# A graph message kernel: comparison ramps and slot masks moved to a PSUM bank, and the transposed one-hots moved to ScalarE

## The chip, the cores and the metric

The kernel runs on one core of one Trainium2 chip. The metric is the device time of one execution in microseconds (us): the median of 3 runs. The engines are called as the profile calls them: PE is TensorE's matmul (PEld its weight loads), DVE is VectorE, ACT is ScalarE, POOL is GpSimd, SP is SyncE, which here only issues DMAs.

## The reference

A graph of 12500 nodes with 64 features each has 800000 edges, each with 4 features of its own, a source and a target node. Every edge makes a message, and the messages are summed by target:

```
h_src = x[src]
h_dst = x[dst]
m_in = jnp.concatenate([h_src, h_dst, e_attr], axis=-1)
h = _silu(m_in @ w1 + b1)            # 132 -> 128
msg = h @ w2 + b2                    # 128 -> 64
return _segment_sum(msg, dst, N)
```

The kernel sums h by target and applies w2 once per node at the end; b2 is multiplied by the number of edges of the node.

## The kernel before, in words

**Tables.** x times the source part of w1 is written to DRAM as a table Atab (one row of two fp16 halves, 512 bytes, per node); x times the target part stays in SBUF as Btab, in buckets of 128 nodes (R = 98 buckets). S, also in SBUF, collects the sums by node.

**Two kinds of work.** The edges come in 16 portions. Each portion is first sorted by bucket of the target (the functions `rank` and `place`, generators that hand out work in small pieces), into rows of CS = 16 edge slots in a DRAM buffer buf. Then the main loop `run` goes over batches of CB = 32 rows (512 slots, two buckets' pieces of 256), one per step, 1590 steps in all. A step belongs to one batch n and works ahead in stages: loads of codes (11 steps ahead), index lists (`sources`, 8), gathers from Atab (`gather`, 6, four indirect DMAs of 128 rows each on GpSimd's queue), the target codes spread over all partitions (`spread`, 4), `targets` (2), `marks` (1), and for n itself `pre` and `silu`, one step later `onehot`, two steps later `seg` and `accum`. While the batches of one portion go through `run`, the sorting of the next portions is put between them as filler: each generator yields a cost in ns with each piece, and `filler` deals the pieces out over the steps and half-steps by these costs. Before the first step the first portion is ranked and placed without anything beside it.

**rank** compares the bucket of each edge with a ramp (ohb, L421, against the ramp iob), counts on TensorE, and gets each edge's place by matmuls into a PSUM tile rx, from which `slots` takes the maximum over the buckets (L529, slT).

**place** works on groups of GT = 20 columns of 128 edges, in pieces of SUB = 5 columns. For each block of 80 columns `records` makes the payload pay (three bf16 parts of the features, the target in its bucket plus one, the source) and per edge the row lo and the slot in the row. For each group the slot becomes a mask over the 16 slots, q, in three passes (L839 shift left, L842 arithmetic shift right by 31, L845 to 16 bits as qh). Per piece, mk is the payload masked by slot: L860 (qh AND pay, 520 32-bit elements) and L864 (q AND the 32-bit pair of target and source, 80 elements). The one-hots oh of the row (L869, one instruction of 384 elements per column, against the ramp io3) and co (L856) go to TensorE as weights; mk is the moving operand, and the product pl holds the rows, which ScalarE copies out (carry, L891; cb, L894) and GpSimd scatters to buf (L878). Later in `rank` the row numbers are found with comparisons stp (L710), also against io3.

**The step.** In `pre` TensorE adds into one PSUM bank px: the gathered rows times idA (L1078), the edge features times WE (L1082), and the target's row of Btab picked by a one-hot oT (L1084). oT is [128, 1024] for two batches: the target codes in the slots, compared on VectorE with the partition number plus one and multiplied by a scale (L1055). `silu` (ScalarE, L1103) gives h; `marks` gives the one-hots the other way round, ob (L1064, against the ramp io1), which ScalarE copies to fp32 (sg, L1099); `seg` (L1111) sums h by target into another px bank, and `accum` (L1119, twice per step, the second as VectorE's last instruction of the step) adds this to S.

**Order.** Each engine works in program order. `in_order` fixes the order of every engine as traced: per step `sources`, `gather`, `spread`, `marks`, `targets`, `seg(n-2)`, `onehot(n-1)`, `pre(n)`, `silu(n)`, then the fillers with TensorE's filler work at four places, with `accum(n-2, 0)` before and `accum(n-2, 1)` after the last of them. Tile buffers rotate: a tile's allocation waits until the user of the same buffer some allocations before has finished. px has 4 banks here, and takes two allocations per step, first `seg(n-2)`, then `pre(n)`; rx and pl have 2 banks each, which makes 8.

```
def targets(n):
    w = st[n]["w"]
    if w:
        oT = st[n]["ot"][:, :512 * w]
        VE.tensor_scalar(oT, oT, iop1[:, 0:1], inv, op0=OP.is_equal, op1=OP.mult)
```

Of the kernel before, what the change touches and what calls it, by code (L numbers as in the profile page):

```python
# [82 lines left out]
def tile_mpnn(ctx, tc, x, e_attr, src, dst, w1, b1, w2, b2, out, portions):  # L83
# [50 lines left out]
    sht = cst.tile([128, CS], I32, name="sht")  # L134
    GP.iota(sht, pattern=[[-1, CS]], base=31, channel_multiplier=0)
    one_i = cst.tile([128, 1], I32, name="one_i")
    GP.memset(one_i, 1)
    ones_b = cst.tile([128, 1], BF, name="ones_b")
# [112 lines left out]
    Btab = cst.tile([128, R, 2, 128], FH, name="Btab")  # L251
    scl = cst.tile([128, 2], F32, name="scl")
    inv = scl[:, 1:2]
# [4 lines left out]
    def tables():  # L258
# [12 lines left out]
        for i, (a, e) in enumerate(zip(qs, qs[1:])):  # L271
# [5 lines left out]
                         apply_absolute_value=True)  # L277
        mp = ps.tile([128, 512], F32, name="px", bufs=4)
        for i in range(3):
# [9 lines left out]
        VE.tensor_scalar(mi[:, 4:5], mi[:, 5:6], -1.0, float(254 << 23), op0=OP.mult, op1=OP.add)  # L289
        sp = ps.tile([128, 512], F32, name="px", bufs=4)  # L290
        PE.matmul(sp[:, 0:2], ones_f[0:1, :], mr[0:1, 4:6], start=True, stop=True)
        VE.tensor_copy(scl, sp[:, 0:2])
        VE.tensor_scalar(idA, idf, inv, None, op0=OP.mult)
        yield 0
        for c0 in range(0, R, 4):
            cn = min(4, R - c0)
            pt = ps.tile([128, 512], F32, name="px", bufs=4)
            for i in range(cn):
# [4 lines left out]
            for i in range(0, cn, 2):  # L303
                m = min(2, cn - i)
                pab = ps.tile([128, 2, 2, 128], F32, name="px", bufs=4)
                for u in range(m):
                    PE.matmul(pab[:, u].rearrange("p a h -> p (a h)"),
                              xt[:65, (i + u) * 128:(i + u + 1) * 128],
                              wab.rearrange("p a h -> p (a h)"), start=True, stop=True)
                for a, hi, lo in ((0, Sh[:, c0 + i:c0 + i + m, :H], Sh[:, c0 + i:c0 + i + m, H:2 * H]),  # L310
                                  (1, Btab[:, c0 + i:c0 + i + m, 0], Btab[:, c0 + i:c0 + i + m, 1])):
                    SC.activation(hi, pab[:, :m, a, :], AF.Copy, scale=scl[:, 0:1])
                    VE.scalar_tensor_tensor(lo, pab[:, :m, a, :], scl[:, 0:1], hi, op0=OP.mult, op1=OP.subtract)
# [434 lines left out]
    def records(p, c0, cn):  # L748
# [6 lines left out]
        def twice(f):  # L755
# [43 lines left out]
                                op0=OP.add, op1=OP.add)  # L799
        tw = wk.tile([128, PW], I32, name="tw")  # L800
        VE.tensor_tensor(tw[:EP, :cn], one_i[:EP].to_broadcast([EP, cn]), kk[:EP, 1, :cn],
                         op=OP.logical_shift_left)
        yield 270
        p["rec", c0] = (pay, lo, tw)
        yield 1200

    def place(p):
# [19 lines left out]
        for c0 in range(0, cols, PW):  # L827
            cn = min(PW, cols - c0)
            if c0 == 0:
                yield from records(p, 0, cn)  # L830
            pay, lo, tw = p.pop(("rec", c0))
            nxt = records(p, c0 + PW, min(PW, cols - c0 - PW)) if c0 + PW < cols else iter(())
            subs = sum(-(-min(GT, cn - go) // SUB) for go in range(0, cn, GT))
            for g in range(c0 // GT, -(-(c0 + cn) // GT)):
                go = g * GT - c0
                gt = min(GT, cn - go)
                assert gt > SUB
                q = wk.tile([128, GT, CS], I32, name="q", bufs=1)
                VE.tensor_tensor(q[:EP, :gt], tw[:EP, go:go + gt].unsqueeze(2).to_broadcast([EP, gt, CS]),  # L839
                                 sht[:EP].unsqueeze(1).to_broadcast([EP, gt, CS]), op=OP.logical_shift_left)  # L840
                yield 735
                VE.tensor_scalar(q[:EP, :gt], q[:EP, :gt], 31, None, op0=OP.arith_shift_right)  # L842
                yield 430
                qh = wk.tile([128, GT, CS], I16, name="qh", bufs=1)
                VE.tensor_copy(qh[:EP, :gt], q[:EP, :gt])  # L845
                yield 300
                for s0 in range(0, gt, SUB):
# [3 lines left out]
                    if s0 + sn == gt:  # L851

                        if s0 < 2 * SUB:
# [6 lines left out]
                    VE.tensor_tensor(  # L860
                        mk[:EP, :sn, CS:].rearrange("p s (f j) -> p s f j", f=NU),
                        qh[:EP, s0:s0 + sn].bitcast(I32).unsqueeze(2).to_broadcast([EP, sn, NU, CS // 2]),
                        pi[:, :, :NU].unsqueeze(3).to_broadcast([EP, sn, NU, CS // 2]), op=OP.bitwise_and)
                    VE.tensor_tensor(mk[:EP, :sn, :CS], q[:EP, s0:s0 + sn],  # L864
                                     pi[:, :, NU:].to_broadcast([EP, sn, CS]), op=OP.bitwise_and)
                    yield 800
# [34 lines left out]
                    def mm(g=g, s0=s0, mk=mk, oh=oh, gt=gt, sn=sn, co=co, at=at):  # L901
                        if s0 == 0:
# [7 lines left out]
                        pa, pb = box[0]  # L910
                        terms = [(oh[:EP, i], mk[:EP, i].bitcast(BF))
                                 for i in range(sn)]
# [35 lines left out]
    def bucket_table(k, t0):  # L948

        tp = ps.tile([128, 512], F32, name="px", bufs=4)  # L950
        ns = 2 * k + 1
# [99 lines left out]
    def targets(n):  # L1051
        w = st[n]["w"]
        if w:
            oT = st[n]["ot"][:, :512 * w]
            VE.tensor_scalar(oT, oT, iop1[:, 0:1], inv, op0=OP.is_equal, op1=OP.mult)  # L1055

# [15 lines left out]
    def pre(n):  # L1072
        s = st[n]
        v = regs(n, ET.PE)
        pr = ps.tile([128, 512], F32, name="px", bufs=4)

# [28 lines left out]
    def seg(n):  # L1105

        s = st[n]
        bank = ps.tile([128, 512], F32, name="px", bufs=4)
# [189 lines left out]
    def turn_sums(b0):  # L1298

        if b0 < R:  # L1300
            bn = min(4, R - b0)
            tp = ps.tile([128, 512], F32, name="px", bufs=4)
            for i in range(bn):
# [53 lines left out]
```

## Time and profile before

| | us |
|---|---|
| median of 3 runs | 9934.91 |
| lowest and highest | 9934.45, 9937.09 |
| the profiled execution | 9947.36 |
| its span, first to last instruction | 9945.5 |
| first gather / last gather of `run` starts | 423.3 / 9880.1 |
| main loop per step, 1590 steps | 5.95 |

A group line of the profile gives line, engine, operation, output<-inputs, shapes and count, then the busy time in us and the mean of one in ns, then the engine's idle time before these instructions and what ended most of it. "issue" is a pause in which the engine waited for nothing that the profile shows. A line of the busy times by stage gives for each stretch its length, then busy us and count of PE, PEld, DVE, ACT and POOL, the granted TensorE clock, the share of the DMA engines and GB/s; asked for one source line, it gives that line's engine alone. A timeline line gives start, duration, engine, line, operation and, in square brackets, the idle time before it. The mean granted TensorE clock of the execution is 0.874.

### The profile page before, as it was taken

What the parts mean: (1) busy time and instruction counts of PE and PEld (TensorE: products, weight loads), DVE (VectorE), ACT (ScalarE), POOL (GpSimd) and SP (SyncE); (2) the same over time, 40 slices, a digit from 0 to 9 for tenths busy, and PEclk for the clock granted to TensorE, in tenths of its full rate; (3) what the DMA queues carried; (4) which work ended last, traced back from release to release, by engine and by line L of the source; (5) the groups of instructions that cost most, each with busy time, mean ns of one, the idle gap of its engine ahead of it and who ended that gap; (6) DMA issues with size and microseconds to landing.
All of it is one profiled execution on the core that took longest, in us unless ns stands there. A gap on an engine that the chain in (4) does not pass through costs nothing. (4 is left out here: it accounts for less than half of the span.)

```text
span 9945.5 us, 220568 instructions
## 1 busy us (share of the span) xinstructions
PE 7609.8 (77%) x72601; PEld 6386.5 (64%) x72601; DVE 7087.5 (71%) x24824; ACT 2096.2 (21%) x3956; POOL 7372.0 (74%) x7039
## 2 busy tenths in 40 slices
PE   7877787887887778777877777777787787776666
PEld 5666666766766667666666666666566666665555
DVE  8978788977996678777677776676687876553222
ACT  1122121221212212222222222222122222222222
POOL 1477777777767777777777777777777777777775
PEclk8988899988988888888888888888898888887777
DMA  1254444544444444444444444454454444544554
GB/s 47 49 93 85 84 81 85 91 78 88 73 79 80 79 88 81 79 90 81 80 88 79 77 90 82 78 93 81 73 96 80 88 77 74 85 80 82 88 86 76
DMA packets 3266044, 806.39 MB, mean 81 GB/s; under 512 B 2979003, under 2 KB 3056216, under 8 KB 3264952
## 3 DMA queue, kind: packets, MB, share of 16 engines
q1 hardware_dynamic: 3038362, 348.44, 28.5%
q0 software_dynamic: 223584, 441.40, 17.1%
q8 instruction: 640, 10.49, 0.5%
q14 instruction: 452, 3.70, 0.1%
q10 hardware_dynamic: 3006, 2.36, 0.1%
HBM read 720.89 MB, written 89.76 MB: 82 GB/s over the span
## 5 line engine op out<-in xcount | busy, mean ns | idle before, releaser
L1092 POOL DMA_INDIRECT ga<-Atab,ix x6360 | 6653.2, 1046 | 1987.1 <-issue 1553.6
L920 PE MATMUL pl<-mk,oh 128*128 128x240 bf16 x18750 | 2401.4, 286 | 124.0 <-DVE oh L869 117.8
L1078 PE MATMUL px<-ga,idA 128*128 128x512 f16 x3180 | 1094.4, 430 | 1685.5 <-DMA ga<-Atab,ix 1137.0
L1103 ACT ACTIVATE h<-px 128x512 f32<-128x512 f32 x1590 | 949.4, 597 | 6756.3 <-PE px L1084 6552.7
L920 PEld LDWEIGHTS <-oh 128*128 128x128 bf16 x18750 | 1917.8, 105 | 459.4 <-DVE oh L869 198.9
L1111 PE MATMUL px<-h,sg 128*128 128x129 f32 x12720 | 1951.0, 300 | 111.4 <-ACT sg L1099 71.1
L1111 PEld LDWEIGHTS px<-h,sg 128*128 128x128 f32 x12720 | 1726.3, 210 | 130.6 <-ACT sg L1099 75.4
L869 DVE TENSOR_SCALAR oh<-io,lo 128x384 bf16<-128x384 bf16 x6250 | 1744.1, 323 | 0.1
L1084 PE MATMUL px<-Btab,oT 128*128 x12720 | 1535.7, 240 | 0.3
L1119 DVE TENSOR_TENSOR S<-S,px 128x129 f32 x3180 | 896.3, 282 | 859.6 <-PE px L1111 785.5
L1078 PEld LDWEIGHTS <-idA 128*128 128x128 bf16 x3180 | 324.6, 102 | 1805.5 <-issue 1614.6
L1082 PE MATMUL px<-WE,pts 65*128 65x128 bf16 x6360 | 1371.6, 241 | 0.8 <-DMA pts<-buf 0.8
L1084 PEld LDWEIGHTS <-oT 128*128 128x128 bf16 x12720 | 1150.8, 110 | 246.5 <-issue 90.9
L529 DVE TENSOR_REDUCE slT<-rx 128x5 f32<-128x490 f32 x1250 | 822.1, 660 | 479.9 <-PE rx L521 474.9
L860 DVE TENSOR_TENSOR mk<-qh,pay 128x520 int32<-128x520 int32 x1250 | 867.2, 694 | 385.6 <-PE pl L920 375.0
L1099 ACT ACTIVATE sg<-ob 128x512 f32<-128x512 bf16 x1590 | 992.2, 624 | 102.5 <-DVE ob L1064 102.2
L878 POOL DMA_INDIRECT buf<-cb,idx x626 | 687.7, 1099 | 294.6 <-issue 131.2
L1082 PEld LDWEIGHTS <-pts 65*128 65x128 bf16 x6360 | 686.7, 108 | 235.0 <-issue 77.8
L521 PEld LDWEIGHTS <-selB 82*128 82x128 bf16 x6250 | 437.4, 103 | 284.5 <-issue 160.8
L1064 DVE TENSOR_TENSOR ob<-io,d 128x1024 bf16<-128x1024 bf16 x795 | 551.3, 693 | 84.1 <-DVE d L1062 1.4
L517 PE MATMUL rx<-ohb,triO 128*128 128x490 bf16 x1250 | 498.7, 399 | 115.8 <-DVE slT L529 80.6
L521 PE MATMUL rx<-bT,selB 82*128 82x98 bf16 x6250 | 511.8, 216 | 15.3 <-DVE bT L503 14.2
(233 smaller groups left out, 5638.0 us busy)
## 6 DMA issues: line engine op xcount, KB each, us to landing
oT<-dsc SPq DMA_DIRECT2D x795, 256.0 KB
ga<-Atab,ix POOLq DMA_INDIRECT x6360
pts<-buf SPq DMA_DIRECT2D x2385, 24.0 KB
buf<-zero SPq DMA_DIRECT2D x272, 120.0 KB
psc<-buf SPq DMA_DIRECT2D x795, 4.0 KB
dsc<-buf SPq DMA_DIRECT2D x795, 2.0 KB
pld<-psc SPq DMA_DIRECT2D x795, 4.0 KB
el<-in_e_attr_dram SPq DMA_DIRECT2D x76, 160.0 KB
```

Of the source, the lines that this page charges most:

```text
L521: PE.matmul(xp[:EP, i * R:(i + 1) * R], selB[:NR, s_:s_ + 1].to_broadcast([NR, EP]), bT[g][:NR, :R], start=False, stop=i == n - 1)
L860: VE.tensor_tensor(mk[:EP, :sn, CS:].rearrange("p s (f j) -> p s f j", f=NU), qh[:EP, s0:s0 + sn].bitcast(I32).unsqueeze(2).to_broadcast([ ...
L869: VE.tensor_scalar(oh[:EP, i], io3[:EP], lo[:EP, go + s0 + i:go + s0 + i + 1], None, op0=OP.is_equal)
L920: PE.matmul(pa[:, u, :CS * PC] if u < 2 else pb[:, :CS * PC], oh_[:, u * 128:(u + 1) * 128], mv, **fl)
L1078: PE.matmul(pr.rearrange("p (t h) -> p t h", t=4), idA, s["ga"][:, :, u * H:(u + 1) * H], start=u == 0, stop=False)
L1082: PE.matmul(pr[:, sl], s["pts"][:, sl], WE, start=False, stop=False)
L1084: PE.matmul(pr[:, sl], s["oT"][:, sl], Btab[:, ds(v[t // 2], 1), u, :], start=False, stop=t == 3 and u == 1)
L1092: GP.indirect_dma_start(out=ga[:, t, :], out_offset=None, in_=Atab, in_offset=bass.IndirectOffsetOnAxis(ap=s["ix"][:, t:t + 1], axis=0))
L1099: SC.activation(sg, s["ob"][:, :4].rearrange("p t h -> p (t h)"), AF.Copy)
L1103: SC.activation(hs[n % 3][:, :, :H], st[n]["pr"].rearrange("p (t h) -> p t h", t=4), AF.Silu)
L1111: PE.matmul(s["so"][t // 2], s["sg"][:, t * 128:(t + 1) * 128], hs[n % 3][:, t, :], start=t % 2 == 0, stop=t % 2 == 1)
L1119: VE.tensor_tensor(S[:, ds(v[u], 1), :], S[:, ds(v[u], 1), :], s["so"][u].unsqueeze(1), op=OP.add)
```

## The change

- The ramps io3, io1 and iob move from SBUF tiles to one PSUM bank, fix: ramps by partition are made on VectorE and transposed there by TensorE, once at the start. Every instruction that compares with a ramp (ohb, stp, co, oh, ob) then reads it from PSUM.
- The slot mask is made in another way. m16 is a bf16 one-hot of the slot over 16 slots. For the masking of 32-bit pairs, half is a 32-bit mask over 8 pairs of slots: a comparison of the slot's upper bits (e8) times a value that covers the lower or the upper 16 bits. half is written to the same bank fix. The first instruction on mk masks with half; the second multiplies target and source, as bf16, with m16, 160 elements instead of 80.
- `records` makes the operands for this (s2, hv) in place of the power of two, tw.
- `targets` makes oT on ScalarE, in two passes over the 1024 elements: the absolute value of code minus partition number minus one, then a rectifier that leaves the scale where that is 0, and 0 elsewhere.
- The px tiles share 3 banks instead of 4, since fix takes one.
- The costs that the generators yield change with the instructions.

```
-    io3 = iota("io3", [[1, NLO]], [128, NLO], base=-NLO // 2, dtype=BF)
...
-    iop1 = cst.tile([128, 1], F32, name="iop1")
-    VE.tensor_scalar(iop1, iop, 1.0, None, op0=OP.add)
-    iob = cst.tile([128, R], BF, name="iob")
-    VE.tensor_copy(iob, io128[:, :R])
-
-    io1 = cst.tile([128, 128], BF, name="io1")
-    VE.tensor_scalar(io1, io128, 1.0, None, op0=OP.add)
-
+    nip1 = cst.tile([128, 1], F32, name="nip1")
+    VE.tensor_scalar(nip1, iop, -1.0, -1.0, op0=OP.mult, op1=OP.add)
+    fix = ps.tile([128, 1024], BF, name="fix")
+    io3, io1, iob, half = fix[:, :NLO], fix[:, NLO:NLO + 128], fix[:, NLO + 128:NLO + 128 + R], fix.bitcast(I32)[:, 512 - GT * CS // 2:]
+    for i, off in enumerate([128 * i - NLO // 2 for i in range(NLO // 128)] + [1, 0]):
+        up = tp0.tile([128, 128], BF, name=f"up{i}")
+        VE.tensor_scalar(up, iop.to_broadcast([128, 128]), float(off), None, op0=OP.add)
+        PE.transpose(fix[:, 128 * i:128 * (i + 1)], up, idb)
...
-    b2p = ps.tile([128, 512], F32, name="px", bufs=4)
+    b2p = ps.tile([128, 512], F32, name="px", bufs=3)
...
+        VE.tensor_scalar(scl[:, 2:3], inv, -1.0, None, op0=OP.mult)
...
-        tw = wk.tile([128, PW], I32, name="tw")
-        VE.tensor_tensor(tw[:EP, :cn], one_i[:EP].to_broadcast([EP, cn]), kk[:EP, 1, :cn],
-                         op=OP.logical_shift_left)
-        yield 270
-        p["rec", c0] = (pay, lo, tw)
+        s2 = wk.tile([128, PW, 2], BF, name="s2")
+        VE.tensor_copy(s2[:EP, :cn], kk[:EP, 1, :cn].unsqueeze(2).to_broadcast([EP, cn, 2]))
+        hv = wk.tile([128, 2, PW], F32, name="hv")
+        VE.tensor_scalar(si[:EP, :cn], kk[:EP, 1, :cn], 1, None, op0=OP.logical_shift_right)
+        VE.tensor_scalar(kk[:EP, 1, :cn], kk[:EP, 1, :cn], 1, None, op0=OP.bitwise_and)
+        yield 600
+        VE.tensor_scalar(hv[:EP, 0, :cn], kk[:EP, 1, :cn], -131071.0, 65535.0, op0=OP.mult, op1=OP.add)
+        VE.tensor_copy(hv[:EP, 1, :cn], si[:EP, :cn])
+        yield 400
+        p["rec", c0] = (pay, lo, s2, hv)
...
-                q = wk.tile([128, GT, CS], I32, name="q", bufs=1)
-                VE.tensor_tensor(q[:EP, :gt], tw[:EP, go:go + gt].unsqueeze(2).to_broadcast([EP, gt, CS]),
-                                 sht[:EP].unsqueeze(1).to_broadcast([EP, gt, CS]), op=OP.logical_shift_left)
-                yield 735
-                VE.tensor_scalar(q[:EP, :gt], q[:EP, :gt], 31, None, op0=OP.arith_shift_right)
-                yield 430
-                qh = wk.tile([128, GT, CS], I16, name="qh", bufs=1)
-                VE.tensor_copy(qh[:EP, :gt], q[:EP, :gt])
-                yield 300
+                m16 = wk.tile([128, GT, CS], BF, name="m16", bufs=1)
+                VE.tensor_tensor(
+                    m16[:EP, :gt].rearrange("p g (j t) -> p g j t", t=2),
+                    iob[:EP, :CS].rearrange("p (j t) -> p j t", t=2).unsqueeze(1).to_broadcast([EP, gt, CS // 2, 2]),
+                    s2[:EP, go:go + gt].unsqueeze(2).to_broadcast([EP, gt, CS // 2, 2]), op=OP.is_equal)
+                yield 250
+                e8 = wk.tile([128, GT, CS // 2], F32, name="e8", bufs=1)
+                VE.tensor_tensor(e8[:EP, :gt], iob[:EP, :CS // 2].unsqueeze(1).to_broadcast([EP, gt, CS // 2]),
+                                 hv[:EP, 1, go:go + gt].unsqueeze(2).to_broadcast([EP, gt, CS // 2]), op=OP.is_equal)
+                half_ = half[:EP, :gt * CS // 2].rearrange("p (g j) -> p g j", g=gt)
+                VE.tensor_tensor(half_, e8[:EP, :gt],
+                                 hv[:EP, 0, go:go + gt].unsqueeze(2).to_broadcast([EP, gt, CS // 2]), op=OP.mult)
+                yield 550
...
-                    mk = wk.tile([128, SUB, PW_], I32, name="mk")
-                    pi = pay[:EP, go + s0:go + s0 + sn].rearrange("p s w t -> p s (w t)").bitcast(I32)
+                    mk = wk.tile([128, SUB, CS * PC], BF, name="mk")
+                    P_ = pay[:EP, go + s0:go + s0 + sn]
                     VE.tensor_tensor(
-                        mk[:EP, :sn, CS:].rearrange("p s (f j) -> p s f j", f=NU),
-                        qh[:EP, s0:s0 + sn].bitcast(I32).unsqueeze(2).to_broadcast([EP, sn, NU, CS // 2]),
-                        pi[:, :, :NU].unsqueeze(3).to_broadcast([EP, sn, NU, CS // 2]), op=OP.bitwise_and)
-                    VE.tensor_tensor(mk[:EP, :sn, :CS], q[:EP, s0:s0 + sn],
-                                     pi[:, :, NU:].to_broadcast([EP, sn, CS]), op=OP.bitwise_and)
+                        mk[:EP, :sn].bitcast(I32)[:, :, CS:].rearrange("p s (f j) -> p s f j", f=NU),
+                        half_[:, s0:s0 + sn].unsqueeze(2).to_broadcast([EP, sn, NU, CS // 2]),
+                        P_.rearrange("p s w t -> p s (w t)").bitcast(I32)[:, :, :NU].unsqueeze(3)
+                        .to_broadcast([EP, sn, NU, CS // 2]), op=OP.bitwise_and)
+                    VE.tensor_tensor(
+                        mk[:EP, :sn, :C_E].rearrange("p s (j t) -> p s j t", t=2),
+                        m16[:EP, s0:s0 + sn].unsqueeze(3).to_broadcast([EP, sn, CS, 2]),
+                        P_[:, :, NU:].to_broadcast([EP, sn, CS, 2]), op=OP.mult)
...
-            VE.tensor_scalar(oT, oT, iop1[:, 0:1], inv, op0=OP.is_equal, op1=OP.mult)
+            SC.activation(oT, oT, AF.Abs, bias=nip1[:, 0:1])
+            SC.activation(oT, oT, AF.Relu, scale=scl[:, 2:3], bias=inv)
```

Every other px tile changes from 4 to 3 banks as b2p does.

More of the change, by code (lines that the diff above doesn't have):

```diff
@@ L251, in tile_mpnn @@
     Btab = cst.tile([128, R, 2, 128], FH, name="Btab")
-    scl = cst.tile([128, 2], F32, name="scl")
+    scl = cst.tile([128, 3], F32, name="scl")
     inv = scl[:, 1:2]
@@ L289, in tables @@
         VE.tensor_scalar(mi[:, 4:5], mi[:, 5:6], -1.0, float(254 << 23), op0=OP.mult, op1=OP.add)
-        sp = ps.tile([128, 512], F32, name="px", bufs=4)
+        sp = ps.tile([128, 512], F32, name="px", bufs=3)
         PE.matmul(sp[:, 0:2], ones_f[0:1, :], mr[0:1, 4:6], start=True, stop=True)
-        VE.tensor_copy(scl, sp[:, 0:2])
+        VE.tensor_copy(scl[:, 0:2], sp[:, 0:2])
+        VE.tensor_scalar(scl[:, 2:3], inv, -1.0, None, op0=OP.mult)
         VE.tensor_scalar(idA, idf, inv, None, op0=OP.mult)
@@ L830, in place @@
                 yield from records(p, 0, cn)
-            pay, lo, tw = p.pop(("rec", c0))
+            pay, lo, s2, hv = p.pop(("rec", c0))
             nxt = records(p, c0 + PW, min(PW, cols - c0 - PW)) if c0 + PW < cols else iter(())
@@ L1107, in seg @@
         s = st[n]
-        bank = ps.tile([128, 512], F32, name="px", bufs=4)
+        bank = ps.tile([128, 512], F32, name="px", bufs=3)
         s["so"] = [bank[:, u * (H + 1):(u + 1) * (H + 1)] for u in range(2)]
```

18 lines of the change are left out of this document (7 added, 11 removed).

## The prediction

> **What bounds the kernel now.** I read the page's totals and costliest groups first, then the busy times by stage, then the timeline around single gathers.
>
> ```profile
> PE 7609.8 (77%) x72601; PEld 6386.5 (64%) x72601; DVE 7087.5 (71%) x24824; ACT 2096.2 (21%) x3956; POOL 7372.0 (74%) x7039
> ...
> L1092 POOL DMA_INDIRECT ga<-Atab,ix x6360 | 6653.2, 1046 | 1987.1 <-issue 1553.6
> ...
> L878 POOL DMA_INDIRECT buf<-cb,idx x626 | 687.7, 1099 | 294.6 <-issue 131.2
> ```
>
> No engine looks full. But GpSimd (POOL) has a pause before each of its indirect DMAs in which it waits for nothing: the list of waits has it with its count, and the gathers of the quiet end of the run show the undisturbed duration.
>
> ```profile
> POOL ga L1092 <- issue: 1553.6, 5097, 0.3
> ```
>
> ```profile
> L1092 POOL DMA_INDIRECT ga<-Atab,ix x238: 940/944/1442, 9300.1 to 9599.4; - x119
> ```
>
> So the pause is 1553.6 / 5097 = 0.305 us, and an undisturbed gather takes 0.94 us (minimum/median/maximum 940/944/1442 ns). The busy times by stage (engines PE, PEld, DVE, ACT, POOL, with counts in brackets) then read differently:
>
> ```profile
> 0.00:423.30 423.30, 324.09 (x2615) 242.67 (x2615) 372.91 (x1303) 75.84 (x165) 78.47 (x92) 0.89 0.15 39
> 423.30:3000.00 2576.70, 2061.07 (x21306) 1740.72 (x21306) 2147.18 (x7684) 532.96 (x1008) 1974.92 (x1832) 0.90 0.47 84
> 3000.00:8750.00 5750.00, 4435.57 (x42878) 3745.64 (x42876) 4153.65 (x14502) 1223.18 (x2304) 4457.60 (x4229) 0.88 0.47 83
> 8750.00:9881.50 1131.50, 738.51 (x5478) 609.11 (x5477) 391.00 (x1234) 248.37 (x453) 860.99 (x887) 0.79 0.53 84
> ```
>
> Call them A to D. POOL with its pauses fills 1974.92 + 1832 x 0.305 = 2534 of 2577 us in B, 4457.60 + 4229 x 0.305 = 5747 of 5750 in C, and all of D. In A, before the first gather, VectorE is busy 372.91 of 423.3 us (88%). **So GpSimd sets the pace from 423 us on, and VectorE before that.**
>
> GpSimd's instructions exceed 0.94 us by 1974.92 - 1832 x 0.94 = 253 us in B, 482 in C and 27 in D. The timeline shows when:
>
> ```profile
> 1704.87 0.66 DVE L529 TENSOR_REDUCE slT<-rx 128x5 f32<-128x490 f32 x1
> 1704.94 0.96 POOL L1092 DMA_INDIRECT ga<-Atab,ix  x1 [0.30 <-DMA ga<-Atab,ix]
> ...
> 5004.57 0.94 POOL L1092 DMA_INDIRECT ga<-Atab,ix  x1 [0.30 <-issue]
> ...
> 5008.39 0.69 DVE L1064 TENSOR_TENSOR ob<-io,d 128x1024 bf16<-128x1024 bf16 x1
> ...
> 5008.47 1.43 POOL L1092 DMA_INDIRECT ga<-Atab,ix  x1 [0.30 <-issue]
> ```
>
> Both long VectorE instructions began 0.07 to 0.08 us ahead of a gather and ran on for 0.6 us. The reduce, whose one input lies in PSUM, cost the gather 0.02 us. The comparison, with two SBUF inputs, cost it 0.49: it ended 0.61 us after the gather's start, so the gather stood from some 0.12 us after its start until the other was done. That is the mechanism which the change addresses.
>
> **The change part by part.** First, GpSimd. If an instruction of d us holds up a gather that reaches its sensitive point under it, and a gather starts each 1.25 us, it costs d x d / 2.5 on average. The durations of before:
>
> ```profile
> L869 DVE TENSOR_SCALAR oh<-io,lo 128x384 bf16<-128x384 bf16 x6250 | 1744.1, 323 | 0.1
> ...
> L860 DVE TENSOR_TENSOR mk<-qh,pay 128x520 int32<-128x520 int32 x1250 | 867.2, 694 | 385.6 <-PE pl L920 375.0 <-issue 1.2
> L529 DVE TENSOR_REDUCE slT<-rx 128x5 f32<-128x490 f32 x1250 | 822.1, 660 | 479.9 <-PE rx L521 474.9 <-issue 1.6 <-PE px L1084 0.4
> L1064 DVE TENSOR_TENSOR ob<-io,d 128x1024 bf16<-128x1024 bf16 x795 | 551.3, 693 | 84.1 <-DVE d L1062 1.4 <-ACT h L1103 0.5
> L421 DVE TENSOR_TENSOR ohb<-iob,bk 128x490 bf16<-128x490 bf16 x1250 | 503.5, 405 | 8.8 <-PE rx L517 7.5
> L1055 DVE TENSOR_SCALAR oT<-oT,iop,scl 128x1024 bf16<-128x1024 bf16 x795 | 446.1, 561 | 23.6 <-DMA oT<-dsc 22.4 <-issue 0.6 <-DMA pts<-buf 0.2
> L864 DVE TENSOR_TENSOR mk<-q,pay 128x80 int32<-128x80 int32 x1250 | 289.9, 232 | 0.0
> ...
> L839 DVE TENSOR_TENSOR q<-tw,sht 128x320 int32<-128x320 int32 x312 | 151.2, 485 | 0.0
> ...
> L845 DVE CAST qh<-q 128x320 int16<-128x320 int32 x312 | 108.6, 348 | 4.6
> L842 DVE TENSOR_SCALAR q<-q 128x320 int32<-128x320 int32 x312 | 105.4, 338 | 2.7
> ...
> L710 DVE TENSOR_SCALAR stp<-io,loc 128x256 bf16<-128x256 bf16 x313 | 90.4, 289 | 174.4 <-PE rx L717 172.1 <-PE px L1084 1.6 <-issue 0.3
> ...
> L782 DVE TENSOR_SCALAR kk<-si 128x80 int32<-128x80 int32 x76 | 15.2, 200 | 0.4
> ```
>
> The two mk run back to back (926 ns): 1250 x 0.343 = 429 us. oh: 6250 x 0.042 = 261. ob 153, oT 100, ohb 82, the q chain 58, stp and co about 45. That is 1128 us of kinds that go, or then read only one operand from SBUF, plus about 130 by the same rule for small ones that stay. Measured are 253 + 482 + 27 = 762, so the rule counts 1.65 times too much (a gather that was held up arrives later at the next). What comes new with two SBUF inputs: the second mk on m16 and pay (1250 x 0.040 = 50) and the product for half (312 x 0.040 = 12). Left are (130 + 62) / 1.65 = 116 of 762 us. **GpSimd sheds 84% of the excess: 212 us in B, 405 in C, 23 in D.** Bounds: nothing, if the excess has another cause, and all 762.
>
> By the Trainium skill (SBUF — State Buffer, Who interferes with whom), an instruction with two tensor inputs does not stall descriptor writing, since it takes only the shared read side. The row at 5008.47 says otherwise, and the measurement decides; by the page only oh, oT, stp and co would give relief, 0.4 of it.
>
> Second, VectorE. SBUF to SBUF, bf16 with one source goes at (323 - 289) / 128 = 0.27 ns per element, bf16 with two sources at (693 - 405) / 534 = 0.54, 32-bit with two sources at (694 - 232) / 440 = 1.05. No row of before reads bf16 from PSUM. From PSUM the reduce takes 660 ns for 490 f32 elements, (660 - 490 x 1.05) = 145 fixed, as the SBUF ones do: no surcharge for PSUM itself. One port instead of two should halve the single-source rate: 0.54 ns per element, +104 ns on each oh and co, +69 on each stp. Bounds: unchanged (0), and 1.05 ns per element (+300). I take 0.54, the nearest bf16 rate with one port per tensor. ob, ohb stay at 0.54.
>
> The second mk goes from 80 32-bit to 160 elements at 1.05: +84 ns. The q chain of 485 + 338 + 348 = 1171 ns becomes a comparison of 320 at 0.54 (313) and two passes of 160 at 1.05 (316 each): -226. A records block loses one pass and gains five of about 200 to 250 ns: +0.85 us, 76 times. oT leaves VectorE: 561 ns less, 795 times. Per stage I count oh and oT:
>
> ```profile
> 0.00:423.30 423.30, 112.94 (x400) 0.89 0.15 39
> 423.30:3000.00 2576.70, 517.12 (x1877) 0.90 0.47 84
> 3000.00:8750.00 5750.00, 1062.51 (x3783) 0.88 0.47 83
> ```
>
> ```profile
> 423.30:3000.00 2576.70, 115.48 (x208) 0.90 0.47 84
> 3000.00:8750.00 5750.00, 270.78 (x482) 0.88 0.47 83
> ```
>
> The mk, q, records and co run with oh (a fifth, a twentieth, 1/82, a twentieth as often), stp is 898 times in all. A: 400 x 0.104 = 42, and 11 for the rest: +53. B: 195 + 65 - 115 = +144. C: 393 + 116 - 271 = +238.
>
> Third, ScalarE takes oT in two passes.
>
> ```profile
> L1099 ACT ACTIVATE sg<-ob 128x512 f32<-128x512 bf16 x1590 | 992.2, 624 | 102.5 <-DVE ob L1064 102.2 <-DVE beg L650 0.2
> ...
> L894 ACT ACTIVATE cb<-pl 128x480 bf16<-128x480 f32 x313 | 177.6, 567 | 212.1 <-DMA buf<-cb,idx 107.0 <-PE pl L920 105.1
> L891 ACT ACTIVATE carry<-pl 98x240 bf16<-98x240 f32 x313 | 115.0, 367 | 504.2 <-PE pl L920 483.0 <-PE rx L717 17.5 <-issue 3.8
> L312 ACT ACTIVATE S<-px,scl 128x256 f16<-128x256 f32 x49 | 23.3, 475 | 46.0 <-PE px L307 45.6
> ```
>
> At (567 - 367) / 240 = 0.83 ns per element 1024 elements take 624 + 427 = 1051, and each operand by pointer about 95 more (475 against 380 for 256): 1.15 + 1.24 = 2.39 us, 795 times. ScalarE goes from 2096 to 3996 us, 40%. Behind the pair in its queue stand sg, the silu and the copies of carry and cb; oT is made two steps ahead of its use, so ScalarE's idle time hides it. I cost it at nothing; without that cover each oT that is late holds TensorE by up to 2.39 us.
>
> Fourth, three banks. pre(n) then takes the bank of seg(n-3) and waits for the second accumulate of step n-3, VectorE's last work in step n-1; TensorE's other work of the step is queued behind it. With four banks it waits hardly at all:
>
> ```profile
> PE px L1078 <- DVE S L1119: 80.4, 16, 23.9
> ```
>
> ```profile
> L1078 PE MATMUL px<-ga,idA 128*128 128x512 f16 x3180 | 1094.4, 430 | 1685.5 <-DMA ga<-Atab,ix 1137.0
> ```
>
> TensorE idles 1685.5 / 1590 = 1.06 us per step at this place, mostly for the gather, and most of the new wait lies in that. I take 25 us for B, where VectorE runs behind TensorE. Bounds: 0, and the rival below.
>
> **The sum.** VectorE's ceiling is about 90% over a long stage; its densest stretch holds 95% while POOL (196.97 + 175 x 0.305 = 250) stays full:
>
> ```profile
> 2500.00:2750.00 250.00, 213.71 (x2232) 183.68 (x2230) 238.05 (x837) 51.39 (x100) 196.97 (x175) 0.95 0.42 73
> ```
>
> A: +53, as VectorE is its bound. B: VectorE 2147 + 144 = 2291, at 90% 2546 us, above GpSimd's 2577 - 212 = 2365: VectorE takes over, -31, and with the banks -6. C: VectorE 4154 + 238 = 4392, at 90% 4880; GpSimd 5345 still sets the pace, but not in every stretch, and the bank wait adds to that: I take three quarters of 405, -304. D: -23. Together -280. The profiled execution took 9947.4 us (span 9945.5), so 9667; it lies 12.4 above the median of the runs, 9934.9, so I forecast **9655 us**.
>
> **The rivals.**
> *The whole of GpSimd's gain arrives.* VectorE holds 95% and the banks cost nothing: B at 2291 / 0.95 = -165, C -405: 53 - 165 - 405 - 23 = -540, 9395. For it: the stretch above. Against: VectorE must be fed evenly.
> *Three banks couple TensorE to VectorE* (the slower side). A step takes 5.95 us (9458 / 1590), 1.06 of it TensorE's idle time at pre. If the wait for the accumulate is over 1.06 us on average, nothing that GpSimd saves counts: at 1.1 us, 64 + 53 - 12 over the profile, about 10050. For it: VectorE is 83% busy in B and grows. Against: 80.4 us of such waits now, and 72% in C.
> *Comparisons of two sources fall to one element per cycle with an operand in PSUM.* ob +533 ns x 795, ohb +255 x 1250, m16 +167 x 312: +795 us of VectorE. With as many ob as oT and a fifth of oh for ohb, C has 4392 + 464 = 4856, at 91% 5336: of its gain some 200 us are left in an uneven load; B with 2291 + 249 at 91% takes 2791, +214; A +78, D -23: about 10000 in all. The Trainium skill speaks for it (VectorE: DVE Perf Modes, The perf-mode tier table, which has 1x for such an instruction with any PSUM operand) and against it (Vector Engine (DVE) Microarchitecture Reference, Performance modes, where element size and step alone decide). No row of before can say.
> *Every bf16 read from PSUM goes at 1.05.* oh and co +196 ns more x 6563, stp +131 x 898, the 795 of the rival before and the 435 of A to C: 2634 us on 6674, and VectorE bounds all up to C's end: 9308 / 0.91 + 1196 = 11400.
> *The excess is not VectorE's doing:* POOL keeps it, A loses 53 and the banks cost 25: about 10010. The timeline speaks against it.
>
> **How the numbers follow.** Forecast (9560 to 9740) 0.46; more of GpSimd's gain (9390 to 9560) 0.16; less, by banks or VectorE (9740 to 9915) 0.13; within 0.2% (some 20 us, about what a measurement of this kernel tells from no change) 0.04; slower 0.21, of it banks 0.08, two-source comparisons 0.07, all PSUM reads 0.04, no relief 0.02. Faster is 0.46 + 0.16 + 0.13 = 0.75. The range 9430 to 10020 leaves out 0.05 below, and 0.09 above.
>
> **What would show it.** The gathers' mean falls from 1046 to about 960 ns; oh rises to about 427 ns and ob stays at 693; two ScalarE rows on oT of 1.15 and 1.24 us, with no table load among them; TensorE's idle time at pre moves from the gather to S. Wrong would make it: oh at 600 or ob at 1200 ns, gathers still at 1.04 us, or a wait of over 1 us per step of px for S.

## The result, and the profile after

| | before | after |
|---|---|---|
| median of 4 runs, us | 9934.7 | 9506.9 |
| lowest to highest, us | 9933.8 to 9937.1 | 9502.4 to 9510.6 |
| ratio | | 0.957, 95% interval 0.955 to 0.959 |

The changed kernel is 428 us faster. The forecast was 280 us faster, 9655; its range reached down to 9430.

These are the totals and the two groups of indirect DMAs of the kernel after, from the page, and the pause before the gathers from its list of waits:

```profile
PE 7439.3 (78%) x72529; PEld 6192.6 (65%) x72606; DVE 7342.5 (77%) x24356; ACT 3891.7 (41%) x5546; POOL 6732.1 (71%) x7036
...
L1101 POOL DMA_INDIRECT ga<-Atab,ix x6360 | 6069.9, 954 | 2109.7 <-issue 1558.7
...
L886 POOL DMA_INDIRECT buf<-cb,idx x626 | 632.8, 1011 | 378.3 <-ACT carry L899 174.4
```

```profile
POOL ga L1101 <- issue: 1558.7, 5115, 0.3
```

GpSimd is busy 640 us less (7372.0 to 6732.1) with the same instructions; the pause of 1558.7 / 5115 = 0.305 us before each is as it was. VectorE is busy 255 us more, ScalarE 1796 more. The granted TensorE clock is 0.899 on the mean, against 0.874.

To compare stage with stage, the cuts are put at the same gathers as before: the first one, 1648 gathers on, and 3851 further on. The busy times of the kernel after by these stages (us and count of PE, PEld, DVE, ACT, POOL):

```profile
0.00:475.60 475.60, 336.75 (x2620) 232.23 (x2620) 409.93 (x1326) 74.86 (x164) 67.90 (x89) 0.94 0.13 35
475.60:2974.50 2498.90, 2042.57 (x21270) 1697.02 (x21289) 2251.45 (x7566) 1003.20 (x1423) 1761.89 (x1832) 0.92 0.49 87
2974.50:8328.10 5353.60, 4261.81 (x42840) 3602.06 (x42893) 4303.54 (x14238) 2308.96 (x3266) 4061.25 (x4230) 0.91 0.52 89
8328.10:9439.30 1111.20, 750.24 (x5473) 615.73 (x5475) 355.00 (x1126) 488.14 (x664) 841.11 (x886) 0.78 0.54 86
```

| stage | before | after | difference | forecast |
|---|---|---|---|---|
| A, to the first gather | 423 | 476 | +52 | +53 |
| B, 1648 gathers | 2577 | 2499 | -78 | -6 |
| C, 3851 gathers | 5751 | 5354 | -397 | -304 |
| D, the last 861 gathers | 1129 | 1110 | -19 | -23 |

C is full of GpSimd as it was before: 4061.25 + 4230 x 0.305 = 5351 of 5354 us, and so is D. B is not: 1761.89 + 1832 x 0.305 = 2321 of 2499, 93%, while VectorE is busy 2251 us, 90%. So after the change GpSimd sets the pace in C and D; in B no engine fills the stage, and VectorE has come close to GpSimd. What B answers to, the experiments show.

The mechanism itself, as a gather meets ob in the kernel after, from its timeline:

```profile
5900.40 0.69 DVE L1073 TENSOR_TENSOR ob<-fix,d 128x1024 bf16<-128x1024 bf16 x1
5900.49 0.94 POOL L1101 DMA_INDIRECT ga<-Atab,ix  x1 [0.30 <-issue]
```

ob began 0.09 us ahead of the gather and lasted 0.69 us, as the pair of the kernel before at 5008.39 and 5008.47 did. There the gather took 1.43 us; with the ramp in PSUM it takes its bare 0.94. Counted over the two whole traces it is the same: of the gathers that started 0.05 to 0.25 us after an ob, all 273 took 1.28 us or more before, and none of 227 took more than 1.01 us after.

The moved instructions on VectorE and ScalarE, from the groups of instructions:

```profile
L877 DVE TENSOR_SCALAR oh<-fix,lo 128x384 bf16<-128x384 bf16 x6250 | 2260.2, 407 | 0.0
...
L865 DVE TENSOR_TENSOR mk<-fix,pay 128x520 int32<-128x520 int32 x1250 | 865.3, 692 | 283.9 <-PE pl L928 278.0
...
L1073 DVE TENSOR_TENSOR ob<-fix,d 128x1024 bf16<-128x1024 bf16 x795 | 550.0, 692 | 214.4 <-ACT sg L1108 141.3 <-DVE d L1071 2.3 <-issue 1.6
L417 DVE TENSOR_TENSOR ohb<-fix,bk 128x490 bf16<-128x490 bf16 x1250 | 503.2, 405 | 9.6 <-PE rx L513 7.8
L870 DVE TENSOR_TENSOR mk<-m,pay 128x160 bf16<-128x160 bf16 x1250 | 395.2, 316 | 0.0
L706 DVE TENSOR_SCALAR stp<-fix,loc 98x256 bf16<-98x256 bf16 x585 | 177.2, 342 | 0.0
...
L849 DVE TENSOR_TENSOR fix<-e,hv 128x160 int32<-128x160 f32 x312 | 104.3, 334 | 10.0
L840 DVE TENSOR_TENSOR m<-fix,s 128x320 bf16<-128x320 bf16 x312 | 98.7, 316 | 0.0
...
L846 DVE TENSOR_TENSOR e<-fix,hv 128x160 f32<-128x160 bf16 x312 | 97.9, 314 | 0.0
```

```profile
L1064 ACT ACTIVATE oT<-oT,scl 128x1024 bf16<-128x1024 bf16 x795 | 986.4, 1241 | 26.7
...
L1063 ACT ACTIVATE oT<-oT,nip 128x1024 bf16<-128x1024 bf16 x795 | 907.8, 1142 | 268.0 <-DMA oT<-dsc 267.8
```

Two-source comparisons (ob 692 ns, ohb 405) and the AND for mk (692) are what they were from SBUF. The one-source oh goes from 323 to 407 ns, stp from 288 to 342 (its 98x256 form).

### The profile page after: what moved, and what is told of

It reads as the page before. It is cut to its first block, busy times and chain, and to the rows that moved or that the text cites. A ratio compares the mean times of both kernels' runs of the same rounds, so it can differ in the third digit from the quotient of the medians.

```text
span 9500.6 us, 220797 instructions
## 1 busy us (share of the span) xinstructions
PE 7439.3 (78%) x72529; PEld 6192.6 (65%) x72606; DVE 7342.5 (77%) x24356; ACT 3891.7 (41%) x5546; POOL 6732.1 (71%) x7036
## 5 line engine op out<-in xcount | busy, mean ns | idle before, releaser
L1101 POOL DMA_INDIRECT ga<-Atab,ix x6360 | 6069.9, 954 | 2109.7 <-issue 1558.7
L928 PE MATMUL pl<-mk,oh 128*128 128x240 bf16 x18750 | 2339.6, 280 | 167.4 <-DVE oh L877 157.6
L877 DVE TENSOR_SCALAR oh<-fix,lo 128x384 bf16<-128x384 bf16 x6250 | 2260.2, 407 | 0.0
L928 PEld LDWEIGHTS <-oh 128*128 128x128 bf16 x18750 | 1820.7, 103 | 514.1 <-DVE oh L877 244.3
L1093 PE MATMUL px<-Btab,oT 128*128 x12720 | 1465.6, 234 | 0.3
L865 DVE TENSOR_TENSOR mk<-fix,pay 128x520 int32<-128x520 int32 x1250 | 865.3, 692 | 283.9 <-PE pl L928 278.0
L1063 ACT ACTIVATE oT<-oT,nip 128x1024 bf16<-128x1024 bf16 x795 | 907.8, 1142 | 268.0 <-DMA oT<-dsc 267.8
L1064 ACT ACTIVATE oT<-oT,scl 128x1024 bf16<-128x1024 bf16 x795 | 986.4, 1241 | 26.7
L886 POOL DMA_INDIRECT buf<-cb,idx x626 | 632.8, 1011 | 378.3 <-ACT carry L899 174.4
L1073 DVE TENSOR_TENSOR ob<-fix,d 128x1024 bf16<-128x1024 bf16 x795 | 550.0, 692 | 214.4 <-ACT sg L1108 141.3
```

The lines of the kernel that those rows point to most:

```text
L877: VE.tensor_scalar(oh[:EP, i], io3[:EP], lo[:EP, go + s0 + i:go + s0 + i + 1], None, op0=OP.is_equal)
L928: PE.matmul(pa[:, u, :CS * PC] if u < 2 else pb[:, :CS * PC], oh_[:, u * 128:(u + 1) * 128], mv, **fl)
L1063: SC.activation(oT, oT, AF.Abs, bias=nip1[:, 0:1])
L1064: SC.activation(oT, oT, AF.Relu, scale=scl[:, 2:3], bias=inv)
L1093: PE.matmul(pr[:, sl], s["oT"][:, sl], Btab[:, ds(v[t // 2], 1), u, :], start=False, stop=t == 3 and u == 1)
L1101: GP.indirect_dma_start(out=ga[:, t, :], out_offset=None, in_=Atab, in_offset=bass.IndirectOffsetOnAxis(ap=s["ix"][:, t:t + 1], axis=0))
```

## The experiments

The ratio is to the kernel before on the same chip, with its 95% interval; "on the scale" means this ratio times 9934.7 us. The kernel before itself had medians of 9932 to 9959 us beside these runs (11925 in the last part), so small differences on the scale are uncertain. A to D are the stages of one profiled execution of each kernel, cut at the same gathers and not scaled, so they need not add up to the difference on the scale. The theory behind the expectations: GpSimd sets the pace wherever it is full; it is held up by VectorE instructions with two SBUF inputs and by one-source comparisons from SBUF to SBUF; and from the start to some 3000 us the price of the change is paid by VectorE.

### Three banks alone

```
-    ... name="px", bufs=4)
+    ... name="px", bufs=3)      (all px tiles of the kernel before, nothing else)
```

> The kernel before with three px banks in place of four and nothing else. My theory: the wait of pre(n) for the accumulate of step n-3 lies inside the time that TensorE waits for gathers anyway, so 9935 us within 20. The rival (three banks couple TensorE to VectorE) expects over 9960, up to 10050, with the wait of px for S well above the 80 us of before.

Measured: ratio 0.9995 (0.9985 to 1.0005), so 9930 on the scale. The wait of pre for the accumulate, from the list of waits of this run:

```profile
PE px L1078 <- DVE S L1119: 87.4, 31, 22.7
```

Before it was 80.4 us in 16 waits. The loss of the fourth bank costs nothing here, and the rival of the three banks falls. In the changed kernel, too, this wait is only 88.3 us in 33 waits.

### oT alone on ScalarE

```
-            VE.tensor_scalar(oT, oT, iop1[:, 0:1], inv, op0=OP.is_equal, op1=OP.mult)
+            SC.activation(oT, oT, AF.Abs, bias=iop1[:, 0:1])          (iop1 now -1 - partition)
+            SC.activation(oT, oT, AF.Relu, scale=scl[:, 2:3], bias=inv)
```

> The kernel before, with only oT moved to ScalarE in two passes; ramps and masks stay in SBUF, four banks. My theory (the time is GpSimd's, and it loses what VectorE's instructions with the second SBUF port cost it): the share of oT in the excess is 100 of 1258 parts of 762 us, so some 60 us less: 9875 (9850 to 9900), gathers 1046 to about 1037 ns. Rival one (what counts is that VectorE has 446 us less to do): a large part of the 428 us that the whole change brought, 9700 or less. Rival two (ScalarE's passes come late and hold TensorE): above 9935.

Measured: ratio 0.992 (0.991 to 0.994), 9858 on the scale. The time is in the stated band, but the reason is only half right: the gathers' mean went to 1042 ns, not 1037, and GpSimd's busy time fell by 31 us (7372.0 to 7341.1), not 60. The profiled execution of this kernel was 40 us shorter than that of the kernel before, of which A to D give -3, -16, -24 and +2. It was the slowest of the four, 23 us above their median, so the stages account for 40 of the 77 us on the scale, and where the rest lies is not shown. VectorE had 362 us less to do (7087.5 to 6725.2); so that relief by itself is worth little while GpSimd is full, and rival one falls; so does rival two, since the time fell.

### The ramp of ob back in SBUF

```
+    io1 = cst.tile([128, 128], BF, name="io1")
+    VE.tensor_scalar(io1, io128, 1.0, None, op0=OP.add)      (after the loop that fills fix)
```

> The changed kernel with the ramp of ob alone back in SBUF: ob then has two SBUF inputs again and keeps its 692 ns. My theory: the excess of the gathers grows by 153 parts of 1258 in 762 us, 93 us, of which those after 3000 us count fully and those before only where GpSimd sets the pace: 9575 to 9600, gathers 954 to about 968 ns. The rival (an instruction with two SBUF inputs does not hold up descriptor writing, only those that read one tensor through both ports do): 9507 within 15, gathers unchanged.

Measured: ratio 0.966 (0.965 to 0.968), 9598 on the scale, 91 us above the changed kernel. The gathers' mean is 968 ns. The timeline has the encounter again, with two SBUF inputs:

```profile
5333.43 0.69 DVE L1075 TENSOR_TENSOR ob<-io,d 128x1024 bf16<-128x1024 bf16 x1
...
5333.52 1.44 POOL L1103 DMA_INDIRECT ga<-Atab,ix  x1 [0.30 <-DVE d L1073]
```

ob is as long as in the changed kernel, it starts 0.09 us ahead of the gather as there, and the gather takes 1.44 us in place of 0.94. It is where the second input lies that costs it, since nothing else differs. In the whole trace all 221 gathers that started 0.05 to 0.25 us after an ob took 1.26 us or more. The rival falls. B and C of this run:

```profile
476.20:2993.50 2517.30, 2049.03 (x21305) 1705.45 (x21304) 2252.20 (x7566) 1002.66 (x1423) 1782.39 (x1833) 0.92 0.51 86
2993.50:8411.80 5418.30, 4294.38 (x42875) 3622.97 (x42876) 4308.83 (x14237) 2309.44 (x3266) 4126.03 (x4230) 0.90 0.53 88
```

C is 65 us longer than in the changed kernel, B 18, D 15. In B GpSimd is busy 20 us more and VectorE 1, and the stage is 18 longer: GpSimd's time still counts there.

### The ramp of oh, co and stp back in SBUF

```
+    io3 = iota("io3", [[1, NLO]], [128, NLO], base=-NLO // 2, dtype=BF)      (after the loop that fills fix)
-        mx = wk.tile([128, 8], F32, name="mx", bufs=1)
+        mx = Btab[:, R - 1, 1, 0:16].bitcast(F32)      (a place of 32 bytes that is free at the start)
```

> The changed kernel with the ramp io3 of oh, co and stp back in SBUF (one-source comparisons, at four elements per cycle again). VectorE gets some 700 us less to do, GpSimd's excess grows by 306 parts of 1258 in 762 us = 185. My theory: the start returns to 423 us (-45), the stage to 3000 us is VectorE's and gains some 100, the stage after it is GpSimd's and loses some 115: 9465 (9420 to 9560). The rival that one-source comparisons are the main cause of the excess (the two-source ones none) expects the gathers' excess nearly all back, over 9700.

Measured: ratio 0.958 (0.956 to 0.959), 9515 on the scale: the changed kernel's time within the intervals. The stages are not the same. From this run:

```profile
437.70:2900.90 2463.20, 2026.03 (x21293) 1715.18 (x21293) 2075.27 (x7566) 1003.21 (x1423) 1824.46 (x1833) 0.91 0.51 88
2900.90:8363.30 5462.40, 4305.61 (x42895) 3658.66 (x42894) 3979.54 (x14241) 2312.41 (x3266) 4169.48 (x4229) 0.90 0.52 87
```

A loses 38 us of its extra, B 36, and C is 109 longer. A and C came as expected (-45, +115). B did not (-100 expected): relieved VectorE falls to 84% there, but GpSimd's excess returns too, 1824.46 + 1833 x 0.305 = 2384 of 2463 us, so that it takes over at once. For these three instructions the move to PSUM gains 109 us in C and costs 74 in A and B; in whole runs that is a gain of 8 us on the scale, within the intervals.

### A mixture: oh from SBUF early, from PSUM later

```
-                        VE.tensor_scalar(oh[:EP, i], io3[:EP], lo...
+                        VE.tensor_scalar(oh[:EP, i], (io3s if k <= 6 else io3)[:EP], lo...
```

io3s is a copy of the ramp in SBUF; portions 0 to 6 are the ones placed in A and B. The changed kernel ran beside it.

> The changed kernel as it is, once more beside another. In the call before, the kernel before itself took 11925 us and the changed one 12125, on a chip on which TensorE pauses without a visible cause (profile: the longest waits end with TensorE's own late start). My theory of the change holds where GpSimd sets the pace: on a chip on which the kernel before takes about 9935 to 9960, the ratio is 0.957 (0.953 to 0.961). If this chip is again one of about 11925, the ratio is again over 1.

> The changed kernel, with oh read from a ramp in SBUF for the portions 0 to 6 only. Where the kernel before takes about 9935: 9435 (9410 to 9470) by my theory (VectorE sets the pace up to 3000 us, GpSimd after), a ratio of 0.950; the rival that GpSimd or the three banks hold the stage up to 3000 us expects only the 38 us of the start, 9470 or more.

Measured: the changed kernel 0.957 (0.956 to 0.959) again, 9508.9 us; the mixture 0.950 (0.949 to 0.952), 9440.7 us. The expectation was 9435. From the mixture's run:

```profile
0.00:442.10 442.10, 330.81 (x2620) 248.34 (x2620) 380.90 (x1327) 73.58 (x164) 73.64 (x91) 0.93 0.14 37
442.10:2908.90 2466.80, 2022.35 (x21271) 1709.85 (x21271) 2106.82 (x7555) 1001.04 (x1421) 1808.96 (x1833) 0.91 0.51 88
2908.90:8263.50 5354.60, 4289.07 (x42921) 3618.40 (x42919) 4308.64 (x14254) 2309.76 (x3268) 4062.33 (x4229) 0.91 0.53 89
```

A and B are those of the run with the ramp in SBUF (442 and 2467 against 438 and 2463), C is that of the changed kernel (5355 against 5354). The stages add up, and this version beats both kernels. The expectation was itself put together from the stages of the run before, so it shows that they add up and no more. In B VectorE has 145 us less to do than in the changed kernel and GpSimd 47 more, and the stage is 32 shorter.

### The old masks

The changed kernel with tw, q, qh and both mk as in the kernel before; everything else as changed.

```
-    m16, e8, half; mk from half (PSUM) and from m16 (SBUF)
+    q, q >> 31, qh; mk from qh and from q (SBUF)
```

> The changed kernel with the slot masks made and applied as in the kernel before (q, qh, both mk from SBUF), ramps in PSUM, oT on ScalarE, three banks, where the kernel before takes about 9935. My theory: some 255 us more excess in all (mk pair 429 and q chain 58 against 62, of 1258 parts of 762 us), two thirds of it after 3000 us where it counts fully; VectorE has about 100 us less to do up to there. 9650 to 9720, gathers near 0.99 us. The run on the other chip showed the gathers at 978 ns, half of that excess, so the rival (the rule of length squared counts the pair too high) expects 9570 to 9630.

Measured: ratio 0.975 (0.973 to 0.977), 9681 on the scale, gathers 989 ns. GpSimd is busy 242 us more than in the changed kernel (6974.6 against 6732.1; 255 expected). B is 43 us longer, C 156:

```profile
473.40:3015.20 2541.80, 2057.60 (x21305) 1703.80 (x21304) 2225.64 (x7466) 1002.58 (x1423) 1834.73 (x1833) 0.91 0.50 85
3015.20:8524.40 5509.20, 4343.74 (x42864) 3651.06 (x42865) 4263.03 (x14035) 2310.57 (x3264) 4217.11 (x4229) 0.90 0.51 86
```

The masks are the dearest part of the old arrangement. The granted clock of this run is 0.892, near the changed kernel's 0.899, and yet it is 174 us slower on the scale: the higher clock alone does not make the kernel faster. The lower estimate, which leant on the gathers' mean of the run on another chip (below), was wrong.

### oT back on VectorE

```
-            SC.activation(oT, oT, AF.Abs, bias=nip1[:, 0:1])
-            SC.activation(oT, oT, AF.Relu, scale=scl[:, 2:3], bias=inv)
+            VE.tensor_scalar(oT, oT, nip1[:, 0:1], inv, op0=OP.is_equal, op1=OP.mult)      (nip1 now partition + 1)
```

> The changed kernel with oT back on VectorE, SBUF to SBUF, where the kernel before takes about 9935. The run on the other chip showed the gathers at 956 ns only (954 in the changed kernel), so oT costs GpSimd some 15 us, not 60. My theory then: VectorE has 115 us more to do in the stage to 3000 us, which it sets, so some 100 there, and about 15 after it: 9600 (9560 to 9650). The rival (ScalarE's passes cost as much as they save) expects 9507 or less.

Measured: ratio 0.963 (0.961 to 0.965), 9567 on the scale, 60 us above the changed kernel: in the band, but otherwise divided than expected. B is 40 us longer (100 expected), C 35 (15 expected): GpSimd is busy 52 us more, as the first estimate of 60 had it, and again the other chip's 956 ns misled; here they are 962. From this run:

```profile
475.60:3015.00 2539.40, 2069.08 (x21292) 1713.07 (x21292) 2340.37 (x7763) 532.78 (x1008) 1775.71 (x1832) 0.91 0.50 85
3015.00:8403.50 5388.50, 4298.25 (x42890) 3605.81 (x42889) 4524.61 (x14729) 1223.26 (x2304) 4095.34 (x4229) 0.90 0.53 88
```

In B VectorE has 89 us more to do, and the stage is only 40 longer: VectorE fills 2340 of 2539 us, 92%, so 90% is no ceiling. ScalarE's two passes thus save more than they cost.

### Four runs on a chip with another bound

Four of these kernels ran first on a chip on which the kernel before takes 11925 us. The expectations were:

> The changed kernel as it is, beside the others of this call on one chip, to compare them with. Ratio to the kernel before 0.957 (9507 us on the scale of 9935).

> The changed kernel, with oh read from a ramp in SBUF for the portions 0 to 6 only (those placed before about 3000 us) and from PSUM for the later ones. My theory: up to 3000 us VectorE sets the pace, so the shorter oh pays there, after it GpSimd does, so the ramp in PSUM pays there: the start gains the 38 us and the stage to 3000 us the 36 us that the run with io3 in SBUF showed, and the stage after keeps the changed kernel's time: 9507 - 70 = 9435 (9410 to 9470), faster than both kernels. The rival that the stage to 3000 us is held by the three banks or by GpSimd expects only the 38 us of the start: 9470 or more.

> The changed kernel with the slot masks made and applied as in the kernel before (q, qh, both mk from SBUF), ramps in PSUM, oT on ScalarE, three banks. My theory: the two mk back to back hold gathers up for 429 parts of 1258 in 762 us again and the q chain for 58, against 62 that go: some 255 us more excess in all, two thirds of it after 3000 us where it counts fully; VectorE has about 100 us less to do up to there. 9650 to 9720, gathers near 0.99 us. The rival (an instruction with two SBUF inputs counts no more than its own overlap, not squared with its length) expects half of that, 9570 to 9600.

> The changed kernel with oT back on VectorE, SBUF to SBUF. My theory: 60 us more excess (some 40 of it after 3000 us), and VectorE has 115 us more to do in the stage to 3000 us, which it sets at about 90%: 9507 + 40 + 100 = 9650 (9590 to 9700). The rival (ScalarE's passes cost as much as they save, since TensorE waits for them) expects 9507 or less.

Measured, as ratios to that 11925: the changed kernel 1.017 (1.014 to 1.019), with the early oh from SBUF 1.013 (1.010 to 1.015), with the old masks 1.017 (1.014 to 1.020), with oT on VectorE 1.020 (1.017 to 1.023). None of the expectations holds there, because their ground is missing. The changed kernel's stage C on that chip (first gather at 476 us as elsewhere):

```profile
3690.10:10705.30 7015.20, 5020.38 (x42907) 4002.32 (x42962) 4350.10 (x14250) 2312.89 (x3269) 4057.22 (x4230) 0.82 0.42 68
```

GpSimd does the same 4057 us of work in 7015, and with its pauses fills 5347 of them. VectorE and ScalarE do the same work, too (4350 and 2313 us against 4304 and 2309). TensorE is busier, 5020 us against 4262, at a granted clock of 0.82 against 0.91. Its timeline shows gaps between its own instructions with nothing to wait for (the bracket at the end of a line):

```profile
5000.30 0.21 PE L517 MATMUL rx<-bT,selB 82*128 82x98 bf16 x1 [1.19 <-issue]
5001.71 0.40 PE L1120 MATMUL px<-h,sg 128*128 128x129 f32 x2 [1.20 <-issue]
5003.84 0.37 PE L1120 MATMUL px<-h,sg 128*128 128x129 f32 x1 [1.73 <-issue]
```

So there TensorE's own pace is the likely bound, and saving GpSimd's time buys nothing: with the old masks, which cost 174 us on the scale elsewhere, the time is the same. What holds TensorE up there stays open, and so does most of the 1.7% that the change costs on that chip: if stage A is some 52 us longer there too, that is a quarter of the 199, and no run there tried four banks. That rival was cleared only where GpSimd sets the pace.

## Why the prediction was right, and where it was not

**GpSimd sets the pace and is held up by VectorE's SBUF reads: right, and sized right.** The excess over 0.94 us is now 1761.89 - 1832 x 0.94 = 40 us in B, 85 in C and 8 in D: 133 of 762 are left, where the forecast had 116. The parts stand as the d x d rule divided them:

| part undone | GpSimd busier, us | forecast |
|---|---|---|
| masks | 242 | 255 |
| oh, co, stp | 178 | 185 |
| ob | 100 | 93 |
| oT | 52 | 60 |

Each is the run's POOL total less the changed kernel's 6732.1. Together they make 573 of the 640 us; ohb was not tried by itself. From the other side it came out lower: oT taken away from the kernel before saved 31 us, not 60.

**What a read from PSUM costs: right.** It is (407 - 342) / 128 = 0.51 ns per element for one source (0.54 was forecast), with no loss for two: ob and ohb are unchanged to 1 ns, so the rival of the two-source comparisons and that of all reads fall. The 1x that the Trainium skill's table (VectorE: DVE Perf Modes, The perf-mode tier table) has for a two-source instruction with any PSUM operand does not hold for bf16 here: ob takes 692 ns, 693 from SBUF. Its Vector Engine (DVE) Microarchitecture Reference, Performance modes, which asks for two-byte elements at step 1 and not for SBUF, does hold.

**VectorE's added work: the first term that was mis-sized.** The forecast had 53 + 144 + 238 = +435 us in A to C; measured are 37 + 104 + 150 = +291, with +104 in B (2147 to 2251). An oh was put at 104 ns more. The rows of both kernels for oh (minimum/median/maximum):

```profile
L869 DVE TENSOR_SCALAR oh<-io,lo x6250: 293/310/1821, 141.6 to 9024.4; 128x384 bf16<-128x384 bf16 x196
```

```profile
L877 DVE TENSOR_SCALAR oh<-fix,lo x6250: 396/408/731, 190.2 to 8577.8; 128x384 bf16<-128x384 bf16 x196
```

The median rises by 98 ns, the mean by only 84 (323 to 407): before, some oh took up to 1821 ns, since VectorE was held up by GpSimd as well, and that tail is gone. The sum counted GpSimd's waits only. With the 2251 us that VectorE really had to do in B, the forecast's own ceiling of 90% gives 2501 us; measured are 2499. That this fits so well is luck, since B does not follow VectorE alone, as the table below shows.

**"I take three quarters of 405" in C: the step that failed.** C gained 397. The quarter that was held back for uneven stretches and for the bank wait did not exist: at 4303 / 5354 = 80% VectorE leaves GpSimd full through the whole stage. The runs with one part undone show it again. Each number is the difference from the changed kernel in us:

| part undone | C: GpSimd busier | C longer | B: GpSimd busier | B: VectorE busier | B longer |
|---|---|---|---|---|---|
| masks | 156 | 156 | 73 | -26 | 43 |
| oh, co, stp | 108 | 109 | 63 | -176 | -36 |
| ob | 65 | 65 | 20 | 1 | 18 |
| oT | 34 | 35 | 14 | 89 | 40 |

In C the time follows GpSimd's busy time to 1 us, up to a VectorE that is 4524.61 / 5388.5 = 84% busy. In B, where VectorE is 84 to 92% busy in these runs, it answers to both engines, and to each by a part. So "VectorE takes over" at 90% in B was too simple a rule.

The shortfall of the forecast is 93 us in C, the quarter, and 72 in B: 25 for the banks, which three banks alone showed to be nothing, and 2546 - 2501 = 45 from VectorE's work that was put too high, as far as the rule of 90% goes.

**Stage A: right by its number, in part by luck.** It is +52 against +53, but VectorE's work there grew by 37 us (372.91 to 409.93), not 53. With oh, co and stp back on SBUF the first gather still starts at 437.7 us, 14 later than before; what these 14 us are stays open. Three banks alone are not it (422.8).

**ScalarE: right.** The passes take 1.14 and 1.24 us against 1.15 and 1.24, and cost less than they save. TensorE's idle time at pre fell with the gathers, as the forecast said it would, but did not move to the accumulates:

```profile
L1087 PE MATMUL px<-ga,idA 128*128 128x512 f16 x3180 | 1064.1, 420 | 1146.0 <-DMA ga<-Atab,ix 621.2 <-DVE ix L1036 195.5 <-DVE S L1128 88.3
```

## What to carry to other kernels

An engine at 74% can be the bound: count the pauses that its instructions always have, and see whether busy time plus pauses fills the stage. Where GpSimd issues indirect DMAs beside VectorE, a VectorE operand in PSUM in place of SBUF kept the gathers from being held up here, at no price for the two-source bf16 instructions (692 ns for ob either way) and at half the rate for the one-source ones (0.51 against 0.27 ns per element); so move the latter only in stages that GpSimd bounds, as the mixture shows. And a stage that one engine fills passed a saving on in full here while the next engine was at most 84% busy (C), and only in part with it at 84 to 92% (B): do not hold back a part of it on suspicion, and do not expect a sharp change of bound either.

## What the runs showed that was not expected

- The hold-up works both ways: VectorE's one-source oh lost about 13 ns each on average to GpSimd (mean 323, median 310 ns). Under a gather an oh took up to 0.56 us. The 1.82 us of the longest stood beside a GpSimd memset of 1.61 us before the first gather.
- The order decides. A gather that starts 0.05 to 0.25 us after an ob with two SBUF inputs is held until ob is done: of the 273 in the kernel before, 263 ended some 0.82 us after ob and ten later still, though the Trainium skill (SBUF — State Buffer, Who interferes with whom) infers that such an instruction leaves descriptor writing alone. Of the 312 gathers that had started up to 0.6 us before ob, or less than 0.05 us after its start, none took more than 1.03 us.
- The same program took 9507 and 9509 us in two sets of runs and 12125 on another chip, where TensorE paused between its own instructions and its granted clock was 0.819 in place of 0.899; the order of the two kernels turned round there.
